# Larger batches in an attention and Fourier kernel: five and six steps, one of them held back through SBUF

## The chip, the cores and the metric

One core of a Trainium2 chip. The metric is the device time of one launch in microseconds (us), the median of three runs. Engines as the profile names them: PE is TensorE's matmul (PEld its weight load), DVE VectorE, ACT ScalarE, POOL GpSimd, SP SyncE.

## The reference

Two independent parts, joined on the last axis. A is attention with 16 query heads of 28 and a single key and value head; B is a Fourier filter over both axes of a 2048 x 448 array.

```python
q = (x @ wq).reshape(B, S, H, Dh).transpose(0, 2, 1, 3)     # S 2048, D 448, H 16, Dh 28
k, v = x @ wk, x @ wv
p = softmax(einsum("bhqd,bkd->bhqk", q, k) * Dh ** -0.5)
a = einsum("bhqk,bkd->bhqd", p, v).transpose(0, 2, 1, 3).reshape(B, S, H * Dh) @ wo
y = irfft2(rfft2(x2) * (w_r + 1j * w_i))
return concatenate([a, y], axis=-1)
```

## The kernel before

The first 70 us project queries, keys and values and do the first Fourier stage; the change does not touch them. Then comes the loop. Queries are cut into four column blocks `c` of 512 and the heads into four groups `g` of four, keys into 16 blocks `kc` of 128. A **step** is one (c, g, kc): 256 in all. It has four **scores** (L780), one 128x512 matmul into a PSUM bank for each head of the group, four exps on ScalarE (L781) from the bank into a buffer `p` in SBUF, and the **value products** in `flush` (L756), four matmuls of 32 columns of `vs` that lie side by side in TensorE's array, accumulated over the 16 steps of a group in one bank `po`. In the trace a value product has two records, so eight a step. The sums of the exps come along as row 28 of each head's 32 rows.

The steps come in **batches** (`PLAN`): the scores of all steps of a batch, then the value products of the steps that are old enough. `KEEP = 2` says that two steps stay pending. Pieces of other work, **units**, are written into the score part: A and B (`fft2_a`, `fft2_b`, three matmuls L519 to L521 each: second Fourier stage), Z (`fft3_a`, `fft3_b`: third stage), W (`wo_unit`, L677: output projection), F (the end of the first stage). The batch lists are A, B, BACK (three steps and a unit), CHUNK (four steps and four W), PAIR and ONE.

Eight PSUM banks serve scores, units and `po`. TensorE's and VectorE's orders are the order of the program text (`manual_schedule`), ScalarE's is left to the scheduler. `take` hands out the oldest free bank, and a score must wait until its bank's last exp or copy is through.

VectorE copies the units' results out of PSUM, makes the products with the filter in `fft2_a` (L565 to L568) and splits them into a high and a low part (`ph`, `pl`), builds the next query block (`build_q`), splits the output weights (`wo_split`) and divides by the softmax sums (`norm`): a copy of `po`, then four times a shuffle that spreads row 28 over the 32 rows, a reciprocal over 128 columns, a product and a high and low part.

Of the kernel before, what the change touches and what calls it, by code (L numbers as in the profile page):

```python
# [21 lines left out]
DH = D // H  # L22
# [10 lines left out]
P_BUFS = 12  # L33
# [4 lines left out]
def batch(*units):  # L38

    return [("----" + u) if i else ("---" + u + "-") for i, u in enumerate(units)]  # L40
# [8 lines left out]
ROOM = {"A": 0, "B": 2, "W": 2, "Z": 2, "": 1, "F": 0}  # L49

KEEP = 2
# [4 lines left out]
def kernel(ctx: ExitStack, tc: tile.TileContext, t: dict):  # L56
# [139 lines left out]
    def build_q(c, g, first=False):  # L196
        cs = slice(c * CW, (c + 1) * CW)
        qh = qp.tile([128, CW], F32R, name="qh", bufs=1)
        ql = qp.tile([128, CW], F32R, name="ql", bufs=1)
        qt = ql.bitcast(F32)  # L200
        nc.vector.tensor_scalar(qt, qraw[:, g, cs], mask, cvec[:, g, c:c + 1], op0=ALU.mult, op1=ALU.add)
        nc.vector.tensor_copy(qh, qt)
        nc.vector.tensor_tensor(ql, qt, qh.bitcast(F32), op=ALU.subtract)
        if (c, g) not in qa:
            qa[c, g] = qp.tile([128, 4, CW], F32R, name="qa")
        q = qa[c, g]
        if first:
            return q, qh, ql
        for i in range(4):
            for p, src in enumerate((qh, ql)):  # L210
                mv = nc.sync.dma_start(q[32 * p:32 * p + 32, i].bitcast(F32), src[32 * i:32 * i + 32].bitcast(F32))
                behind(mv, stored[-1])
        nc.sync.dma_start(q[64:128].bitcast(F32), q[0:64].bitcast(F32))
# [263 lines left out]
    ctx.enter_context(tc.manual_schedule(engines={mybir.EngineType.DVE}))  # L477
# [5 lines left out]
    take, late = free.popleft, []  # L483

    def give(bank, scores=1):

        late.append([scores, bank])

    def scored(bank):
        free.append(bank)  # L490
        for x in late:
            x[0] -= 1
        free.extend(bank for n, bank in late if n == 0)
        late[:] = [x for x in late if x[0]]
    ap = pools.enter_context(tc.tile_pool(name="ap", bufs=2))
    pp = pools.enter_context(tc.tile_pool(name="pp", bufs=P_BUFS))

# [12 lines left out]
    def wo_split(g):  # L510
        if g >= NG:
            nc.vector.tensor_copy(wox[:, g - NG], wo[g])
            return
        nc.vector.tensor_copy(woh[:, g], wo[g])
        nc.vector.tensor_tensor(wol[:, g], wo[g], woh[:, g].bitcast(F32), op=ALU.subtract)

# [28 lines left out]
    def fft2_split(u):  # L545
        q, v = divmod(u, 2)
        b = b2["b", q][:, 2 * v:2 * v + 2]
        bh = b2["h", u] = fp.tile([128, 2, DF], F32R, name="bh", bufs=1)
        nc.vector.tensor_copy(bh, b.bitcast(F32))
        nc.vector.tensor_tensor(b, b.bitcast(F32), bh.bitcast(F32), op=ALU.subtract)  # L550

    def fft2_a(u):
        q, v = divmod(u, 2)
        s = slice(2 * v, 2 * v + 2)
        b, wr, wi = (b2[n, q][:, s] for n in ("b", "wr", "wi"))
        bank = take()
        pu = halves2(bank)
        mm3(pu, "g1", b2["h", u], b)
        us = fp.tile([128, 2, DF], F32, name="us", tag="us", bufs=1)
        nc.vector.tensor_copy(us, pu)  # L560
        give(bank)
        if u < 15:
            fft2_split(u + 1)
        pf, p2 = fp.tile([128, 2, DF], F32, name="pwr"), fp.tile([128, 2, DF], F32, name="pwi")
        nc.vector.tensor_tensor(pf, us, wr, op=ALU.mult)  # L565
        nc.vector.tensor_tensor(p2[0:64], us[64:128], wi[64:128], op=ALU.mult)
        nc.vector.tensor_tensor(p2[64:128], us[0:64], wi[0:64], op=ALU.mult)
        nc.vector.scalar_tensor_tensor(pf, p2, sgn, pf, op0=ALU.mult, op1=ALU.add)  # L568
        h = fp.tile([128, 2, DF], F32R, name="ph")
        nc.vector.tensor_copy(h, pf)  # L570
        p = fp.tile([128, 2, DF], F32R, name="pl")
        nc.vector.tensor_tensor(p, pf, h.bitcast(F32), op=ALU.subtract)
        pr[u] = h, p

    def fft2_b(u):
        v = u % 2
        bank = take()
        pc = halves2(bank)
        mm3(pc, "g2", *pr.pop(u))
        if v == 0:  # L580
            cst[0] = fp.tile([128, 4, DF], F32, name="cst")
        nc.vector.tensor_copy(cst[0][:, 2 * v:2 * v + 2], pc)
        give(bank)
# [22 lines left out]
    def fft3_a(q, e):  # L606
# [3 lines left out]
        for j in range(4):  # L610
            mm(pz[:w, j], c2["c", q][:, j, o0:o0 + w], c2["F", q][:, j], start=True, stop=True)  # L611
        z = c2["z", q, e] = fp.tile([113, 2, 4, 64], F32, name=f"z{e}", tag=("wi", "cst")[e])
        nc.vector.tensor_copy(z[:w], pz[:w].rearrange("p j (r n) -> p r j n", r=2))
        give(bank)

    def fft3_b(q, v):
# [5 lines left out]
        for k, (z, w, r) in enumerate(((ze, 113, 0), (zo, 112, 0), (zo, 112, 1), (ze, 113, 1))):  # L622
            mm(py[:, k], z[:w, r, js], cs3[:w, k], start=True, stop=True)  # L623
        m = fp.tile([128, 4, 113], F32, name="m", tag="us", bufs=1)
        nc.vector.tensor_copy(m, py)  # L625
        give(bank)
        y1 = fp.tile([128, 2, 2, 113], F32, name="y1", tag="pwr")
        nc.vector.tensor_tensor(y1[:, :, 0], m[:, 0:2], m[:, 2:4], op=ALU.add)
        nc.vector.tensor_tensor(y1[:, :, 1], m[:, 0:2], m[:, 2:4], op=ALU.subtract)
        yo = fp.tile([128, 4, 113], F32, name="yo", tag="pwi")  # L630
        nc.gpsimd.tensor_tensor(yo[:, 0:2], y1[:, 0], y1[:, 1], op=ALU.add)  # L631
        nc.gpsimd.tensor_tensor(yo[:, 2:4], y1[:, 0], y1[:, 1], op=ALU.subtract)
        r0 = (2 * q + v) * 128
        nc.sync.dma_start(t["ob"][r0:r0 + 128], yo)
# [14 lines left out]
    def norm(c, g, k):  # L649

        if k == 0 and g == 0:
            oh[c] = pp.tile([128, NG, CW], F32R, name="oh", bufs=1)
            ol[c] = pp.tile([128, NG, CW], F32R, name="ol", bufs=1)
        s = slice(128 * k, 128 * k + 128)
        o = osb[c, g][:, s]
        r = ap.tile([128, 128], F32, name="r", bufs=1)
        nc.vector.stream_shuffle(r, o, [DH] * 32)
        nc.vector.reciprocal(r, r)  # L658
        if c < NC - 1:
            nc.vector.tensor_tensor(o, o, r, op=ALU.mult)  # L660
        else:
            nc.vector.scalar_tensor_tensor(o, o, mask, r, op0=ALU.mult, op1=ALU.mult)
        if (c, g) == (NC - 1, NG - 1):
            return
        h = oh[c][:, g, s]
        nc.vector.tensor_copy(h, o)
        nc.vector.tensor_tensor(ol[c][:, g, s], o, h.bitcast(F32), op=ALU.subtract)
        if k == 3 and c < NC - 1:
            spares(c, g)
# [9 lines left out]
    def wo_out(p, c, k, on_act=False):  # L679
# [3 lines left out]
        else:  # L683
            nc.vector.tensor_copy(y, p)  # L684
        r0 = c * CW + k * 128
# [4 lines left out]
    def wo_unit(c, k, g):  # L690
        if g == 0:
            wps[c, k] = take()
        p = wps[c, k][:, :D]
        wo_mm(p, c, k, (g,))
        if g == NG - 1:
# [17 lines left out]
    place, where, room = [], {}, []  # L713
    for b, steps in enumerate(PLAN):
        for i, s in enumerate(steps):
            for k in s.replace("-", ""):
                where.setdefault(k, []).append(len(place))
            place.append((b, i))
        units = "".join(steps).replace("-", "")
        room.append(ROOM[units[:1]])  # L720
# [14 lines left out]
    builds = set()  # L735
    for g in range(NC * NG - 1):
        n = next(n for n in range(16 * g + 3, 16 * g + 13) if place[n][1] < 2 and room[place[n][0]])
        builds.add(n)
        room[place[n][0]] -= 1

# [6 lines left out]
    pend, po = [], {}  # L747
    step = 0

    def flush(keep, last=False):  # L750
        while len(pend) > keep:
            c, g, kc, ps = pend.pop(0)
            if kc == 0:
                po[c, g] = take()
            for i in range(4):
                mm(po[c, g][32 * i:32 * i + 32], vs[:, kc], ps[i // 2][:, i % 2], start=(kc == 0), stop=(kc == 15))  # L756
            if kc == 15:
                o = osb[c, g] = ap.tile([128, CW], F32, name="osb")
                if last:
                    for k in range(4):  # L760
                        s = slice(128 * k, 128 * k + 128)
                        nc.scalar.activation(o[:, s], po[c, g][:, s], AF.Copy)
                else:
                    nc.vector.tensor_copy(o, po[c, g])
                    give(po[c, g])
                    norms.extend((c, g, k) for k in range(4))

    for c, g in order:
        for kc in range(16):
            ps, n = [], 0  # L770
            b, i = place[step]
            for k in PLAN[b][i]:
                if k != "-":
                    f, *a = todo[k].popleft()
                    f(*a)
                    continue
                if n % 2 == 0:
                    ps.append(pp.tile([128, 2, CW], F32, name="p"))
                sc = take()
# [238 lines left out]
```

## Time and profile before

| | |
|---|---|
| median of 3 runs | 651.04 us (650.68 to 651.18) |
| profiled execution: span | 649.8 us |
| TensorE, matmul busy | 642.6 us |
| ScalarE busy | 555.9 us |
| VectorE busy | 360.5 us |
| GpSimd busy | 79.6 us |
| granted TensorE clock | full in every slice |

Busy times are unions of overlapping records; matmuls are pipelined, so the time from one start to the next is what an instruction costs, not its own length. In the chain of work that ended last, a row gives start, length, engine, tile, line and count. In a timeline row the bracket at the end gives the idle time before and what ended it. A row of a group gives busy time and the mean of one in ns, then idle time before it and who ended that.

### The profile page before, as it was taken

How to read it: one execution, taken by the hardware profiler on the slowest of the kernel's cores; microseconds unless marked ns; L12 is line 12 of the kernel's file. 1: busy time of each engine (PE TensorE's matmuls, PEld its weight loads, DVE VectorE, ACT ScalarE, POOL GpSimd, SP SyncE). 2: the span in 40 equal slices, each digit the busy share in tenths (PEclk: the TensorE clock that was granted, in tenths of full speed). 3: DMA queues.
4: the chain of work that ended last, by engine and by line, in shares of the span. 5: the costliest groups of instructions: out<-in, count | busy, mean ns of one | idle time of the engine just before them, and what ended most of it. 6: DMA issues, size and time to landing. Idle time of an engine off the chain costs nothing.

```text
span 649.8 us, 12076 instructions
## 1 busy us (share of the span) xinstructions
PE 642.6 (99%) x4470; PEld 375.8 (58%) x4470; DVE 360.5 (55%) x810; ACT 555.9 (86%) x1103; POOL 79.6 (12%) x150
## 2 busy tenths in 40 slices
PE   8999999999999999999999999999999999999996
PEld 6877554555555456554546556565656565555555
DVE  5999646778877771047765620175443510383523
ACT  5654999999999998789989988799999987899981
POOL 3022401101112100000012200011120200010010
PEclk9999999999999999999999999999999999999999
DMA  8756954534552443022062323032232313140001
GB/s 268 265 172 165 259 159 106 137 100 121 138 139 76 109 95 84 29 75 49 32 155 50 98 60 89 20 88 73 63 94 61 101 39 84 43 110 16 15 31 60
DMA packets 36114, 63.83 MB, mean 98 GB/s; under 512 B 7905, under 2 KB 23922, under 8 KB 35084
## 3 DMA queue, kind: packets, MB, share of 16 engines
q1 hardware_dynamic: 30832, 49.60, 27.6%
q0 software_dynamic: 4640, 12.48, 7.4%
q8 instruction: 36, 0.59, 0.4%
q10 hardware_dynamic: 576, 0.92, 0.4%
q14 instruction: 30, 0.25, 0.1%
HBM read 30.04 MB, written 14.75 MB: 69 GB/s over the span
## 4 chain that ended last, share of the span: by engine, by line
PE 98%; DMA 1%; ACT 0%; SPq 0%; ACTq 0%; issue 0%
PE s L780 30%; PE s L756 24%; PE po L756 7%; PE s L331 6%; PE sx L780 5%; PE po L780 4%; PE sx L756 4%; PE s L677 4%; PE s L138 2%; PE s L623 2%; PE s L611 1%; PE pbb L157 1%; DMA raw<-wq 1%; PE s L521 1%; PE s L519 1%; PE s L520 1%
## 5 line engine op out<-in xcount | busy, mean ns | idle before, releaser
L781 ACT ACTIVATE p<-s 128x512 f32<-128x512 f32 x776 | 421.9, 652 | 38.8 <-PE s L780 38.5
L780 PE MATMUL s<-qa,ka 128*128 128x512 f32 x776 | 243.8, 408 | 0.0
L780 PEld LDWEIGHTS s<-qa,ka 128*128 128x128 f32 x776 | 140.3, 188 | 80.5 <-ACT p L781 43.6
L756 PE MATMUL s<-p,vs 128*32 128x512 f32 x1408 | 163.8, 596 | 0.0
L756 PEld LDWEIGHTS s<-p,vs 128*32 128x32 f32 x1408 | 39.7, 109 | 89.5 <-issue 86.6
L781 ACT ACTIVATE p<-sx 128x512 f32<-128x512 f32 x132 | 86.1, 652 | 3.4 <-PE sx L780 3.4
L781 ACT ACTIVATE p<-po 128x512 f32<-128x512 f32 x116 | 74.9, 646 | 7.2 <-PE po L780 7.1
L658 DVE RECIPROCAL r<-r 128x128 f32<-128x128 f32 x64 | 61.0, 953 | 2.2
L684 DVE COPY ya<-s 128x448 f32<-128x448 f32 x11 | 6.9, 625 | 88.1 <-PE s L677 88.1
L780 PE MATMUL sx<-qa,ka 128*128 128x512 f32 x132 | 53.4, 405 | 0.0
L780 PE MATMUL po<-qa,ka 128*128 128x512 f32 x116 | 47.4, 408 | 0.0
L756 PE MATMUL po<-p,vs 128*32 128x512 f32 x384 | 44.9, 597 | 0.0
L631 POOL TENSOR_TENSOR yo<-y 128x226 f32<-128x226 f32 x16 | 9.6, 597 | 225.9 <-issue 214.8
L780 PEld LDWEIGHTS sx<-qa,ka 128*128 128x128 f32 x132 | 24.8, 188 | 14.0 <-ACT p L781 9.2
L647 POOL DMA_DIRECT2D ol<-ol x36 | 18.1, 508 | 105.4 <-PE s L780 55.9
L756 PE MATMUL sx<-p,vs 128*32 128x512 f32 x256 | 29.7, 596 | 0.0
L780 PEld LDWEIGHTS po<-qa,ka 128*128 128x128 f32 x116 | 21.8, 188 | 12.4 <-ACT p L781 7.0
L625 DVE COPY m<-s 128x452 f32<-128x452 f32 x15 | 9.4, 629 | 34.5 <-PE s L623 34.5
L756 PEld LDWEIGHTS po<-p,vs 128*32 128x32 f32 x384 | 10.7, 109 | 24.1 <-issue 23.4
L331 PE MATMUL s<-xh,wqh 128*128 128x512 f32 x56 | 22.7, 405 | 0.9 <-ACT wqh L311 0.9
L335 ACT ACTIVATE qraw<-s 128x512 f32<-128x512 f32 x14 | 8.1, 600 | 17.4 <-PE s L331 17.4
L331 PE MATMUL s<-xh,wql 128*128 128x512 f32 x56 | 21.6, 391 | 0.0
(211 smaller groups left out, 735.3 us busy)
## 6 DMA issues: line engine op xcount, KB each, us to landing
qa<-qa SPq DMA_DIRECT2D x15, 512.0 KB
raw<-xa SPq DMA_DIRECT2D x16, 256.0 KB
xb<-xb SPq DMA_DIRECT2D x8, 512.0 KB
qa<-qh SPq DMA_DIRECT2D x64, 64.0 KB
qa<-ql SPq DMA_DIRECT2D x60, 64.0 KB
ob<-yo SPq DMA_DIRECT2D x16, 226.0 KB
t<-bs SPq DMA_DIRECT2D x16, 225.0 KB
wr<-wr POOLq DMA_DIRECT2D x16, 225.0 KB, 4.4
```

The lines of the kernel that those rows point to most:

```text
L138: mm(pa[r0:r0 + 32, e, o0:o0 + n], f[:, 2 * r + k, 2 * p + e, h], cs1[:, 2 * r + k, :n], start=True, stop=True)
L331: mm(pq, w[:, j, gs], x[:, j], start=(j == 0 and n == 0), stop=(j == 3 and n == 1))
L335: out = nc.scalar.activation(qraw[:, g, cs], pq, AF.Copy)
L623: mm(py[:, k], z[:w, r, js], cs3[:w, k], start=True, stop=True)
L625: nc.vector.tensor_copy(m, py)
L631: nc.gpsimd.tensor_tensor(yo[:, 0:2], y1[:, 0], y1[:, 1], op=ALU.add)
L647: nc.gpsimd.dma_start(ol[c][o, g].bitcast(F32), ol[c][r, 0].bitcast(F32))
L658: nc.vector.reciprocal(r, r)
L677: mm(p, x[c][:, g, s], w, start=(g == 0 and n == 0), stop=(g == NG - 1 and n == 2))
L756: mm(po[c, g][32 * i:32 * i + 32], vs[:, kc], ps[i // 2][:, i % 2], start=(kc == 0), stop=(kc == 15))
L780: begun.append(mm(sc, ka[:, kc * 128:(kc + 1) * 128], qa[c, g][:, n], start=True, stop=True))
L781: nc.scalar.activation(ps[-1][:, n % 2], sc, AF.Exp, scale=SCALE)
```

## The change

- `PLAN`: 86 batches become 49. After two batches of one step and four of two, eleven have five steps, 31 have six, and the last has five. A token `-` is a score as before, `k` or `e` one of the last step's four scores, letters are units (`X` is four W, `Y` two Z).
- The last step of a batch of five or six (`k`): VectorE copies the score bank to SBUF (`keep`), and ScalarE does the exps there later, two instructions of 128x1024, behind the exps of the batch. In the batches of one and two steps (`e`) ScalarE takes them from PSUM.
- `flush` comes once a batch: the first step, the step kept from the batch before, then the others. The batch's last step is kept. `P_BUFS` goes from 12 to 8, beside four buffers `k`.
- ScalarE's order is now the program's too. Banks are handed out by clocks that the program keeps for three engines (`clock`, `passed`, `at_once`).
- VectorE's work that nobody waits for at once goes through two queues (`put`, `pop`, `need`) and is issued when VectorE's kept clock is not ahead of TensorE's.
- In `fft2_a` the two half-height products go to GpSimd.
- The division: `po` is transposed in 32x32 blocks on the way out of PSUM, so that a query's sum lies beside its 28 values; one reciprocal over 16 columns, one product, and a transpose back.

```diff
-A, B, BACK = [batch(u, "", "") for u in "ABZ"]
-CHUNK = 4 * [4 * ["--W--"]]
-ONE, PAIR = batch(""), batch("", "")
-PLAN = ([["----F"], ONE] + 4 * [PAIR] + [batch("A", ""), A] + 11 * [B, A] + [PAIR] + CHUNK
-        + 3 * [B, A] + [B, B, PAIR, ONE] + 6 * [BACK] + CHUNK + [PAIR] + 15 * [BACK] + CHUNK + 11 * [BACK])
+PLAN = ["eeeeF", "eeee"] + 4 * [spread(2, "", 0)]
+PLAN += ["-k-k-k-k----------A--"] + [spread(5, u) for u in ["A"] + 9 * ["BA"]]
+PLAN += [spread(6, u) for u in ["BA"] + 4 * ["WBWA"] + 2 * ["WBW"] + ["X"]]
+PLAN += [spread(6, u) for u in 5 * ["Y"] + 4 * ["X"] + 6 * ["Y"] + 4 * ["X"]]
...
+    def passed(work):
+        clock["pe"] += work
+        while any(queue) and clock["dve"] <= clock["pe"]:
+            pop()
+        clock["dve"] = max(clock["dve"], clock["pe"] - 512)
...
         us = fp.tile([128, 2, DF], F32, name="us", tag="us", bufs=1)
         nc.vector.tensor_copy(us, pu)
...
-        nc.vector.tensor_tensor(p2[0:64], us[64:128], wi[64:128], op=ALU.mult)
-        nc.vector.tensor_tensor(p2[64:128], us[0:64], wi[0:64], op=ALU.mult)
+        nc.gpsimd.tensor_tensor(p2[0:64], us[64:128], wi[64:128], op=ALU.mult)
+        nc.gpsimd.tensor_tensor(p2[64:128], us[0:64], wi[0:64], op=ALU.mult)
...
+    def divide(c, g, k=None):
...
+            r = osb["r"] = ap.tile([128, 16], F32, name="r", bufs=1)
+            nc.vector.reciprocal(r, sums[:, :, DH])
...
+        put(("o", c, g), [lambda: divide(c, g), lambda: nc.vector.transpose(o, o),
+                          lambda: nc.vector.tensor_copy(h, o), rest], 640)
...
+            c, g, kc = steps[i if kind == "-" else n - 1]
+            sc = take()
+            begun.append(mm(sc, ka[:, kc * 128:(kc + 1) * 128], qa[c, g][:, h], start=True, stop=True))
+            passed(232)
+            if kind == "-":
+                waiting.append((sc, new[i], h))
+                exps()
+            elif k == "k":
+                nc.vector.tensor_copy(keep[h // 2][:, h % 2], sc)
+                at_once()
+                give(sc)
+                lazy.append(h)
...
+        flush(steps[:1] + kept if n > 4 else kept + steps[:-1], steps[1:-1] if n > 4 else [])
+        kept = steps[-1:]
...
+            for p in keep:
+                nc.scalar.activation(p, p, AF.Exp, scale=SCALE)
```

How the orders move. TensorE, in the A and B batches, before: scores (`s`, `sx`, `po` are banks), a B unit (L519 to L521) and the value products (L756) of three steps.

```order
L520 MATMUL po<-ph,g2l 128x450
L521 MATMUL po<-pl,g2h 128x450
L780 MATMUL s_88<-qa,ka 128x512
L780 MATMUL s_85<-qa,ka 128x512
L780 MATMUL s_89<-qa,ka 128x512
L780 MATMUL sx<-qa,ka 128x512
L780 MATMUL s_86<-qa,ka 128x512
L780 MATMUL s_87<-qa,ka 128x512
L780 MATMUL s_88<-qa,ka 128x512
L780 MATMUL po<-qa,ka 128x512
L780 MATMUL s_85<-qa,ka 128x512
L756 MATMUL s_84<-p,vs 32x512 x12
```

Twelve scores and one unit lie between two runs of value products. The same place in the new order, the end of a batch of five (scores are L875, value products L830, an A unit L557 to L559):

```order
L557 MATMUL sx<-bh,g1h 128x450
L558 MATMUL sx<-bh,g1l 128x450
L559 MATMUL sx<-b_1709,g1h 128x450
L875 MATMUL s_85<-qa,ka 128x512
L875 MATMUL s_87<-qa,ka 128x512
L875 MATMUL s_88<-qa,ka 128x512
L875 MATMUL s_86<-qa,ka 128x512
L875 MATMUL sx<-qa,ka 128x512
L830 MATMUL s_84<-p,vs 32x512 x4
L830 MATMUL s_84<-k,vs 32x512 x4
L830 MATMUL s_84<-p,vs 32x512 x12
```

Twenty scores, a B and an A unit lie between two runs, and a run takes the first step, the kept one (`k`) and three more. The same batch earlier, from its eighth score (the fourth `k`, in bank `po`):

```order
L875 MATMUL po<-qa,ka 128x512
L875 MATMUL s_89<-qa,ka 128x512
L557 MATMUL s_85<-ph,g2h 128x450
L558 MATMUL s_85<-ph,g2l 128x450
L559 MATMUL s_85<-pl,g2h 128x450
L875 MATMUL sx<-qa,ka 128x512
L875 MATMUL s_87<-qa,ka 128x512
L875 MATMUL s_88<-qa,ka 128x512
L875 MATMUL s_86<-qa,ka 128x512
L875 MATMUL s_89<-qa,ka 128x512
L875 MATMUL po<-qa,ka 128x512
```

The bank that VectorE copies last is asked for again by the fifteenth score. VectorE in another batch of five, behind its four score copies (L881), the B unit's copy (`cst`) and the first half of a weight split:

```order
L554 TENSOR_TENSOR wol<-wo,woh 128x448
L602 COPY us<-s_86 128x450
L610 TENSOR_TENSOR pwr<-us,wr 128x450
L588 CAST bh<-b_1484 128x450
L589 TENSOR_TENSOR b_1484<-b_1484,bh 128x450
L614 SCALAR_TENSOR_TENSOR pwr<-pwi,sgn,pwr 128x450
L615 CAST ph<-pwr 128x450
L616 TENSOR_TENSOR pl<-pwr,ph 128x450
L834 STREAM_TRANSPOSE osb<-sx 128x512
L711 RECIPROCAL r<-osb 128x16
L716 TENSOR_TENSOR osb<-osb,r 128x512
L730 STREAM_TRANSPOSE osb<-osb 128x512
```

The two products that stood between L610 and L614 are gone to GpSimd (`pwi`), a division stands behind the unit's chain, and the next batch's copies follow it.

More of the change, by code (lines that the diff above doesn't have):

```diff
@@ L576, in fft2_b @@
         v = u % 2
+        need(("pr", u))
         bank = take()
@@ L732 @@
         at(max(where["Z"][4 * q] - 8, where["B"][-1] + 1), fft3_load, q)
[L735 to L739, printed above, removed]
     norms = deque()
@@ L798 @@
     while norms:
         norm(*norms.popleft())
+    while any(queue):
+        pop()
     c = NC - 1
```

302 lines of the change are left out of this document (186 added, 116 removed).

## Prediction

> **What bounds the kernel now.** I read the page's busy shares first, then the chain of work that ended last.
>
> ```profile
> span 649.8 us, 12076 instructions
> PE 642.6 (99%) x4470; PEld 375.8 (58%) x4470; DVE 360.5 (55%) x810; ACT 555.9 (86%) x1103; POOL 79.6 (12%) x150
> PE 98%; DMA 1%; ACT 0%; SPq 0%; ACTq 0%; issue 0%
> ```
>
> The third row is the chain: TensorE is on it for 98% of the span, so a change pays only if TensorE has less to do or waits less. Busy time does not say whether it runs at its rate, so the next view is the timeline of its matmuls.
>
> ```profile
> 321.42 0.37 PE L519 MATMUL s<-ph,g2h 128*128 128x450 f32 x1
> ...
> 322.03 0.40 PE L780 MATMUL sx<-qa,ka 128*128 128x512 f32 x1
> 322.26 1.33 PE L780 MATMUL s<-qa,ka 128*128 128x512 f32 x5
> 323.43 0.40 PE L780 MATMUL sx<-qa,ka 128*128 128x512 f32 x1
> ```
>
> Five scores take 323.43 - 322.26 = 1.17 us, so 0.234 each; three 450-column matmuls take 322.03 - 321.42 = 0.61. Now the chain in order of time, which shows the value products (L756, eight records a step):
>
> ```profile
> 92.39 1.85 PE s L756 x16
> 97.91 2.71 PE s L756 x24
> 100.62 0.43 PE s L780
> ...
> 249.88 3.57 PE s L756 x32
> 259.63 3.57 PE s L756 x32
> ...
> 317.98 2.71 PE po L756 x24
> 324.30 2.71 PE po L756 x24
> ...
> 620.06 0.88 PE s L623 x8
> ...
> 629.67 4.43 PE s L756 x40
> ```
>
> Two, three, four and five steps cost 1.85, 2.71, 3.57 and 4.43 us: 0.86 a step and a constant of 0.13. The first score behind them takes 0.43 in place of 0.234, another 0.20. A Z unit (L623) takes 0.88. So each run of value products costs **0.33 us** that does no work. The periods agree: a batch of three with one A or B unit is 12 x 0.234 + 0.61 + 3 x 0.86 = 6.00, and the period is 324.30 - 317.98 = 6.32; a batch of four with its eleven output matmuls (L677, taken at the same 0.203) is 3.74 + 2.23 + 3.44 = 9.41, and the period is 9.75. What is left over is 0.32 and 0.34. TensorE waits for nobody in these batches; its only waste is the toll.
>
> **The change part by part.** *Fewer runs.* The old plan has 86 batches and leaves up to two steps pending; its first batch has nothing old enough, so there are 85 runs of L756. The new plan has 49 batches and holds back one step; its first flush is empty and the last follows a run directly, so 48 runs. Scores, units and value products stay in number: 1024 scores, 256 steps, 16 A, 16 B, 48 W, 32 Z. Gain: 37 x 0.33 = **12.2 us**.
>
> *ScalarE.* It must keep up with fewer gaps. A row of exps, and its only instruction of 1024 columns:
>
> ```profile
> 258.23 1.18 ACT L781 ACTIVATE p<-s 128x512 f32<-128x512 f32 x2
> 259.18 0.72 ACT L781 ACTIVATE p<-sx 128x512 f32<-128x512 f32 x1
> 259.66 1.22 ACT L781 ACTIVATE p<-s 128x512 f32<-128x512 f32 x2
> ```
>
> ```profile
> L250 ACT ACTIVATE ka<-kf x1: 1046/1046/1046, 42.4 to 42.4; 32x1024 fp32r<-32x1024 f32 x1
> ```
>
> Three exps start in 259.66 - 258.23 = 1.43 us, 0.477 each. An exp over 1024 columns from SBUF has no row; it lies between two exps back to back, 0.954, and the 1024-column copy with nothing overlapped, 1.046. A new batch of five needs 16 x 0.477 + 2 x 1.046 = 9.7 us at most, against TensorE's 20 x 0.234 + 5 x 0.86 + 2 x 0.61 + 0.33 = 10.5; of six with two Z units 11.6 against 5.6 + 5.2 + 1.8 + 0.3 = 12.9. The deferred exps lie under the value products: in a five-step batch these last 4.4 us, and two of 1.046 follow some four leftover exps (1.9), 4.0 in all. If that cover were gone, the excess of each batch would be paid. I take nothing. The eight score buffers `p` (twelve before) hold four steps; in a six-step batch the fifth step's exps wait for the first step's value product, which is why that one goes first, 3.4 us ahead of the fifth's own. Nothing either.
>
> *VectorE, the term against.* It gains four copies of 128x512 out of PSUM in 43 batches, loses two of its three products per A unit to GpSimd, and its softmax division shrinks.
>
> ```profile
> L658 DVE RECIPROCAL r<-r 128x128 f32<-128x128 f32 x64 | 61.0, 953 | 2.2
> L657 DVE STREAM_SHUFFLE r<-osb 128x128 f32<-128x128 f32 x64 | 19.1, 298 | 0.0
> L764 DVE COPY osb<-s 128x512 f32<-128x512 f32 x10 | 6.9, 690 | 14.7 <-PE s L756 14.7
> L203 DVE TENSOR_TENSOR ql<-ql,qh 128x512 fp32r<-128x512 f32 x16 | 11.3, 709 | 0.5
> ```
>
> The reciprocal over 128 columns four times a group becomes one over 16 columns, about 16/128 x 0.95 = 0.12. The two 32x32 transposes of 128x512 have no row. Below stands the copy at 0.69, above the reciprocal's rate, 4 x 0.95 = 3.8; nearest is the shuffle, which also moves data between partitions and takes 0.298 for 128 columns, the time of a plain elementwise operation of that size. I take 0.65. The freed time lies off the chain and buys nothing by itself. What counts is where VectorE must answer: TensorE wants the copied banks back. The chain of an A unit before:
>
> ```profile
> 108.56 0.63 DVE L560 COPY us<-s 128x450 f32<-128x450 f32 x1 [0.80 <-ACT p L781]
> 109.10 0.39 DVE L549 CAST bh<-b 128x450 fp32r<-128x450 f32 x1
> 109.52 0.63 DVE L550 TENSOR_TENSOR b<-b,bh 128x450 fp32r<-128x450 f32 x1
> 110.07 0.62 DVE L565 TENSOR_TENSOR pwr<-us,wr 128x450 f32<-128x450 f32 x1
> 110.72 0.62 DVE L566 TENSOR_TENSOR pwi<-us,wi 64x450 f32<-64x450 f32 x1
> 111.37 0.62 DVE L567 TENSOR_TENSOR pwi<-us,wi 64x450 f32<-64x450 f32 x1
> 112.03 0.69 DVE L568 SCALAR_TENSOR_TENSOR pwr<-pwi,sgn,pwr 128x450 f32<-128x450 f32 x1
> 112.75 0.40 DVE L570 CAST ph<-pwr 128x450 fp32r<-128x450 f32 x1
> 113.18 0.63 DVE L572 TENSOR_TENSOR pl<-pwr,ph 128x450 fp32r<-128x450 f32 x1
> ```
>
> By starts: the PSUM copy costs 0.54 (its tail overlaps; a 512-column one 0.60), the three operations before the two moved products 0.42 + 0.55 + 0.65 = 1.62, the three behind them 0.72 + 0.43 + 0.63 = 1.78. In the new order L614 stands behind the first three and waits for GpSimd. GpSimd's price:
>
> ```profile
> L631 POOL TENSOR_TENSOR yo<-y x16: 577/584/813, 355.9 to 629.2; 128x226 f32<-128x226 f32 x16
> ```
>
> ```profile
> 355.88 0.81 POOL L631 TENSOR_TENSOR yo<-y 128x226 f32<-128x226 f32 x1 [6.03 <-DVE y L629]
> 356.29 0.69 DVE L202 CAST qh<-ql 128x512 fp32r<-128x512 f32 x1
> 356.66 0.76 POOL L632 TENSOR_TENSOR yo<-y 128x226 f32<-128x226 f32 x1
> 357.01 0.96 DVE L203 TENSOR_TENSOR ql<-ql,qh 128x512 fp32r<-128x512 f32 x1
> ```
>
> At 0.584 for 226 columns, 450 take about 1.1, two 2.2: if nothing interferes, L614 starts 2.3 us after `us` and the chain behind `us` is 2.3 + 1.8 = 4.1 us, against 4.7 before. But the last four rows show the two engines stretching each other: L203 took 0.96 where its mean is 0.71, GpSimd 0.81 and 0.76 where alone it takes 0.58. Run strictly in turn (product 0.65, GpSimd 1.1, cast 0.40, GpSimd 1.1, difference 0.55) the chain is 3.8 + 1.8 = 5.6.
>
> Now the slack. From a batch's first score: the second score's result is there at 0.43 + 0.40 = 0.83, four copies at 0.60 end at 3.2. The fourth copied bank is asked for again behind fourteen scores and B: 0.43 + 13 x 0.234 + 0.61 = 4.1 (`po` in the new TensorE order shown with the change). So a lag up to 0.8 us is free. The batch whose VectorE order is shown with the change: copies to 3.2, `cst` 3.8, a weight split 0.42 + 0.57 to 4.8; `us` waits for A until 5.1 and ends at 5.6; the chain to 9.7 or 11.2; transpose 0.65, reciprocal 0.12, product 0.70, transpose 0.65 to 11.8 or 13.3. The next copies are due at 10.5 + 0.8 = 11.3, so the lag is 0.5 or 2.0 and TensorE stands 0 or 1.2 us. Six of the eleven five-step batches carry such an extra load (a division, a query build or a weight split); counted likewise with full turns they cost 0.3 to 1.4 each, 5.7 together, and 0 with none. Six-step batches add 1.8 us of TensorE time each and absorb it. The rows show stretching, but over pieces only, so I take the middle: **+3 us**, bounds 0 and 5.7.
>
> A rule of the Trainium skill speaks against the move to GpSimd: the page "SBUF — State Buffer", section "Who interferes with whom", says that a VectorE instruction with two SBUF inputs and a GpSimd instruction that reads SBUF exclude each other for the whole instruction. By that rule the cost is the 5.7 end, not 3; the four rows above agree in kind, and only one such meeting is in this trace.
>
> *Start and tail.* The eight-score batches at the start keep their size, and the tail from 629.67 + 4.43 = 634.1 runs the same output matmuls; the last division is ready under the partial sums. Nothing.
>
> Sum: 649.8 - 12.2 + 3.0 = 640.6 us of span. The runs' median is 1.2 above the profiled span (651.04 against 649.8), so **641.8 us**.
>
> **The rivals.** *No stall*: GpSimd's products hide, 649.8 - 12.2 + 1.2 = 638.8. For it: VectorE was busy only 55% of the span. Against: the stretched rows.
>
> *VectorE and GpSimd take turns*: 638.8 + 5.7 = 644.5, up to 647 if the six-step A batches lag by the same half microsecond. The rule quoted above would give this. For it: L203 at 0.96. Against: the overlap there is one meeting.
>
> *The toll is no toll but ScalarE's late release, which grows with the batch.* The page puts the idle weight loads of the scores down to ScalarE:
>
> ```profile
> L780 PEld LDWEIGHTS s<-qa,ka 128*128 128x128 f32 x776 | 140.3, 188 | 80.5 <-ACT p L781 43.6
> ```
>
> If that were the cause, the loss would go with the exps, 85 x 0.33 = 28 us over 256 steps, and longer batches would save none of it: 651.0 + 3 = 654, slower. It decides as soon as the toll of a six-step batch exceeds (28 - 3) / 48 = 0.52 us. Against: runs of two to five steps all show 0.13 + 0.20, and while weight loads stand idle the array is still streaming.
>
> *Slow transposes.* At 3.8 us instead of 0.65, the seven transposes in the five-step batches add 22 us that VectorE, full there, can't hide: 641.8 + 22 = 664. It decides (no gain left) from 0.65 + 9.2 / 7 = 2.0 us each. Against: the shuffle's 0.298.
>
> **How the numbers follow.** Forecast, 640 to 643.5: 0.48. No stall, 638 to 640: 0.20. Turns, 643.5 to 648: 0.20. Toll that grows 0.05, slow transposes 0.04, something within 0.2% of before 0.03. About 0.2% is what a measurement of this kernel can tell from no change. Faster 0.88, same 0.03, slower 0.09. The range 638 to 647 leaves out the slower cases and the end of the turns.
>
> **What would show it.** The chain of waits should list about 48 runs of value products, periods of 10.5 us (A and B), 12.9 (Z) and the same 0.33 left over. The exp over 1024 columns should be near 0.95 and end before the next batch. The transposes near 0.65. A score waiting for VectorE in the batches between 95 and 210 us, of 0.5 to 1.4 us, confirms the term of 3; none there confirms the first rival. Waits for ScalarE in the Z batches, or a first score behind a run that takes much more than 0.43, would make the prediction wrong.

## The result, and the profile after

| | median of its runs | range | runs |
|---|---|---|---|
| before | 651.09 us | 650.58 to 651.58 | 12 |
| changed | 650.75 us | 649.82 to 651.92 | 12 |

The ratio is 0.9994, 95% interval 0.9986 to 1.0002: no change that can be measured. The prediction was 641.8 us with a range of 638 to 647, so it was wrong. Its gain of some 12 us did come, and nearly all of it went out again in three places.

From the page of the changed kernel: span, busy times, the chain that ended last, and three groups (line, engine, operation, shapes, count, then busy time and mean of one in ns, then the idle time before them).

```profile
span 649.4 us, 12044 instructions
PE 639.5 (98%) x4470; PEld 381.7 (59%) x4470; DVE 386.4 (59%) x663; ACT 552.6 (85%) x1013; POOL 121.1 (19%) x182
PE 90%; DVE 7%; DMA 1%; ACT 1%; issue 1%; SPq 0%; ACTq 0%; DVEq 0%
L898 ACT ACTIVATE k<-k 128x1024 f32<-128x1024 f32 x86 | 88.1, 1103 | 0.0
L606 POOL TENSOR_TENSOR pwi<-us,wi 64x450 f32<-64x450 f32 x16 | 23.2, 1448 | 113.3 <-DVE us L602 76.3
L834 DVE STREAM_TRANSPOSE osb<-s 128x512 f32<-128x512 f32 x11 | 7.9, 715 | 38.8 <-PE s L830 38.8
```

TensorE's busy time fell by 3.1 us, the span by 0.4. VectorE, which was not in the chain, now holds 7% of it. The two new operations have the size that was assumed: the transpose 0.715 us (0.65 assumed), and of two 1024-column exps in a row the second starts 0.95 us behind the first (0.95 to 1.05 assumed). GpSimd's products took 1.45 us each (L606), not the 1.1 assumed, and the reciprocal over 16 columns 0.25 (L711, below), not 0.12.

The groups of VectorE, by line:

```profile
L589 DVE TENSOR_TENSOR b<-b,bh 128x450 fp32r<-128x450 f32 x16 | 18.3, 1146 | 0.6
L588 DVE CAST bh<-b 128x450 fp32r<-128x450 f32 x16 | 17.8, 1111 | 0.0
```

These two stand beside the products that moved to GpSimd. Before, the same cast took 0.39 us and the same difference 0.63 in the unit that the prediction showed. What this does to TensorE, from the timelines of TensorE and of VectorE around two of the five-step batches:

```profile
122.98 0.63 PE L875 MATMUL s<-qa,ka 128*128 128x512 f32 x2
124.16 0.50 PE L875 MATMUL s<-qa,ka 128*128 128x512 f32 x1 [0.55 <-DVE k L881]
```

```profile
138.03 0.63 DVE L602 COPY us<-s 128x450 f32<-128x450 f32 x1 [0.35 <-PE s L559]
...
139.24 1.35 DVE L588 CAST bh<-b 128x450 fp32r<-128x450 f32 x1
140.63 1.46 DVE L589 TENSOR_TENSOR b<-b,bh 128x450 fp32r<-128x450 f32 x1
...
143.70 0.71 DVE L834 STREAM_TRANSPOSE osb<-sx 128x512 f32<-128x512 f32 x1
144.44 0.25 DVE L711 RECIPROCAL r<-osb 128x16 f32<-128x16 f32 x1
...
146.09 2.45 DVE L881 COPY k<-s 128x512 f32<-128x512 f32 x4
```

The first fence has a score that starts 1.18 us behind a pair that should take 0.47: it waits for the first of its own batch's four copies to free a bank (that copy ends at 124.11). The second, two batches later, shows how such copies come late: the cast and the difference last 2.8 us together, the division follows, and the four copies of a batch whose first score starts at 143.58 begin at 146.09.

For the whole loop I took, from the matmul starts, each period between two runs of value products and subtracted its work at the prediction's prices (0.234 a score, 0.203 a unit's matmul, 0.88 a Z unit, 0.86 a step, 0.33 toll). What is left, in us, with four of the experiments below beside it (rounding of the prices moves a whole column by up to half a microsecond; differences between columns hold to about 0.2):

| batches | before | changed | e1 | e2 | e6 | e12 |
|---|---|---|---|---|---|---|
| 11 of five steps, A and B | | 6.4 | 2.3 | 6.4 | 1.9 | 0.8 |
| 6 of six steps, A or B and W | | 2.5 | 2.5 | 2.5 | 2.5 | 0.9 |
| 9 of six steps, W | | 0.9 | 0.8 | 0.9 | 0.8 | -0.2 |
| 16 with Z | | 2.5 | 2.6 | 1.1 | 1.1 | -0.2 |
| whole loop | 1.0 | 12.4 | 8.3 | 11.0 | 6.4 | 1.3 |

The loop has 48 runs of value products as predicted, and 37 fewer are worth 37 x 0.33 = 12.2. But waits rose from 1.0 to 12.4 us, 11.4 more. The experiments say what each part of these 11.4 is.

### The profile page after: what moved, and what is told of

Same layout as the page of the kernel before. It is cut to its first block, busy times and chain, and to the rows that moved or that the text cites. A ratio compares the mean times of both kernels' runs of the same rounds, so it can differ in the third digit from the quotient of the medians.

```text
span 649.4 us, 12044 instructions
## 1 busy us (share of the span) xinstructions
PE 639.5 (98%) x4470; PEld 381.7 (59%) x4470; DVE 386.4 (59%) x663; ACT 552.6 (85%) x1013; POOL 121.1 (19%) x182
## 4 chain that ended last, share of the span: by engine, by line
PE 90%; DVE 7%; DMA 1%; ACT 1%; issue 1%; SPq 0%; ACTq 0%; DVEq 0%
PE s L875 28%; PE s L830 22%; PE po L830 6%; PE s L343 6%; PE sx L875 4%; PE po L875 4%; PE s L739 3%; PE sx L830 3%; PE s L141 2%; PE s L672 2%; PE s L658 1%; PE sx L739 1%; PE po L739 1%; DVE bh L588 1%; PE pbb L160 1%; DVE k L881 1%
## 5 line engine op out<-in xcount | busy, mean ns | idle before, releaser
L819 ACT ACTIVATE p<-s 128x512 f32<-128x512 f32 x645 | 344.6, 631 | 40.4 <-PE s L875 33.4
L875 PE MATMUL s<-qa,ka 128*128 128x512 f32 x786 | 238.3, 408 | 2.1 <-DVE k L881 2.1
L875 PEld LDWEIGHTS s<-qa,ka 128*128 128x128 f32 x786 | 144.4, 188 | 76.3 <-issue 30.5
L830 PE MATMUL s<-p,vs 128*32 128x512 f32 x1136 | 134.1, 595 | 0.0
L881 DVE COPY k<-s 128x512 f32<-128x512 f32 x122 | 78.1, 680 | 75.9 <-PE s L875 75.7
L898 ACT ACTIVATE k<-k 128x1024 f32<-128x1024 f32 x86 | 88.1, 1103 | 0.0
L830 PEld LDWEIGHTS s<-p,vs 128*32 128x32 f32 x1136 | 34.4, 109 | 75.1 <-issue 72.2
L819 ACT ACTIVATE p<-sx 128x512 f32<-128x512 f32 x95 | 59.9, 630 | 4.1 <-PE sx L875 3.1
L819 ACT ACTIVATE p<-po 128x512 f32<-128x512 f32 x88 | 55.8, 634 | 6.4 <-PE po L875 4.7
L875 PE MATMUL sx<-qa,ka 128*128 128x512 f32 x121 | 48.8, 403 | 0.0
L875 PE MATMUL po<-qa,ka 128*128 128x512 f32 x117 | 47.4, 405 | 0.0
L606 POOL TENSOR_TENSOR pwi<-us,wi 64x450 f32<-64x450 f32 x16 | 23.2, 1448 | 113.3 <-DVE us L602 76.3
L881 DVE COPY k<-po 128x512 f32<-128x512 f32 x27 | 18.4, 681 | 41.2 <-PE po L875 41.2
L830 PE MATMUL po<-p,vs 128*32 128x512 f32 x312 | 37.2, 595 | 0.0
L830 PE MATMUL s<-k,vs 128*32 128x512 f32 x272 | 35.6, 594 | 0.0
L875 PEld LDWEIGHTS po<-qa,ka 128*128 128x128 f32 x117 | 22.0, 188 | 10.2 <-issue 3.4
L875 PEld LDWEIGHTS sx<-qa,ka 128*128 128x128 f32 x121 | 22.7, 188 | 8.3 <-issue 3.4
L830 PE MATMUL sx<-p,vs 128*32 128x512 f32 x208 | 24.8, 595 | 0.0
L881 DVE COPY k<-sx 128x512 f32<-128x512 f32 x23 | 15.6, 680 | 14.1 <-PE sx L875 14.0
```

The source lines that it names most:

```text
L606: nc.gpsimd.tensor_tensor(p2[0:64], us[64:128], wi[64:128], op=ALU.mult)
L819: nc.scalar.activation(tiles[-1][:, h % 2], sc, AF.Exp, scale=SCALE)
L875: begun.append(mm(sc, ka[:, kc * 128:(kc + 1) * 128], qa[c, g][:, h], start=True, stop=True))
L881: nc.vector.tensor_copy(keep[h // 2][:, h % 2], sc)
L898: nc.scalar.activation(p, p, AF.Exp, scale=SCALE)
```

## The experiments

Theory at the outset: VectorE and GpSimd take turns (A and B batches), a bank is held too long in the Z batches, and the last scores of a batch run short of banks. The main rival was that fewer runs of value products save little. Every ratio is to the kernel before on the same chip.

**e1: the half-height products back on VectorE.**

```diff
-        nc.gpsimd.tensor_tensor(p2[0:64], us[64:128], wi[64:128], op=ALU.mult)
-        nc.gpsimd.tensor_tensor(p2[64:128], us[0:64], wi[0:64], op=ALU.mult)
...
+            lambda: nc.vector.tensor_tensor(p2[0:64], us[64:128], wi[64:128], op=ALU.mult),
+            lambda: nc.vector.tensor_tensor(p2[64:128], us[0:64], wi[0:64], op=ALU.mult)], first=True)
```

> The changed kernel with one thing undone: the two half-height filter products of an A unit go back from GpSimd to VectorE (into the same queue as the third product). Theory 'turns': the 8.9 us that the A and B batches lose (11 five-step batches 0.58 us each above their work, six with W 0.41) come from VectorE and GpSimd excluding each other, L588 and L589 taking 1.3 us in place of 0.4 and 0.6. Then the chain behind us shrinks from about 5.6 to 4.7 us although VectorE does 1.3 us more, the five-step batches go to 10.6 us on average, and the time falls by 5 to 8 us, to 643 to 646. Rival 'load': VectorE is simply full there and the exclusion is hidden; then 1.3 us more per A unit costs 10 us or more, time 660 and up.

Measured: 646.45 us, ratio 0.993 (0.9914 to 0.9947). VectorE does two products more for each A unit, and the kernel is 4.3 us faster. The same stretch of its timeline:

```profile
136.22 0.63 DVE L602 COPY us<-s 128x450 f32<-128x450 f32 x1 [0.35 <-PE s L559]
...
138.79 0.40 DVE L588 CAST bh<-b 128x450 fp32r<-128x450 f32 x1
139.23 0.63 DVE L589 TENSOR_TENSOR b<-b,bh 128x450 fp32r<-128x450 f32 x1
...
142.82 2.48 DVE L882 COPY k<-s 128x512 f32<-128x512 f32 x4
```

The copies start 6.6 us after `us`; in the changed kernel it is 146.09 - 138.03 = 8.1. In the table only the row of the five-step batches falls, by 4.1. VectorE has more work and TensorE waits less, so the turns are shown and the rival 'load' is out; the gain is a little under the 5 to 8 us that were expected.

**e2: `m`, the copy of a Z unit's bank, in two buffers.** A Z unit's copy then need not wait for the additions (`y`) of the unit before it.

```diff
-        need(("y", 2 * q + v - 1))
-        m = fp.tile([128, 4, 113], F32, name="m", tag="us", bufs=1)
+        need(("y", 2 * q + v - 2))
+        m = fp.tile([128, 4, 113], F32, name="m", tag="ph")
```

> The changed kernel, with two buffers in place of one for the tile m into which the fft3_b units are copied, so that the second Z unit's copy need not wait for the queue to be worked off to the first one's sums. Theory 'held bank': the 2.5 us that the 15 six-step Z batches lose come from those with fft3_b units, where the second unit's bank was copied 2.4 us late and the last scores ran at the pace of ScalarE's releases (0.49 us each); the time falls by about 2.5 us. Rival 'ScalarE's pace': eight banks less po are too few for six steps whatever VectorE does; the last scores of the Z batches still stand at 0.49 and the time stays within 0.7 us.

Measured: 649.36 us, ratio 0.9972 (0.9962 to 0.9982), 1.4 less than the change. VectorE behind the two Z units of one batch, in the changed kernel and then in e2:

```profile
467.78 0.63 DVE L676 COPY m<-s 128x452 f32<-128x452 f32 x1 [0.32 <-PE s L672]
468.32 0.68 DVE L209 TENSOR_TENSOR ql<-ql,qh 128x512 fp32r<-128x512 f32 x1
...
470.81 0.63 DVE L676 COPY m<-sx 128x452 f32<-128x452 f32 x1
```

```profile
466.89 0.63 DVE L676 COPY m<-s 128x452 f32<-128x452 f32 x1 [0.32 <-PE s L672]
...
468.03 0.62 DVE L676 COPY m<-sx 128x452 f32<-128x452 f32 x1
```

The second unit's bank comes back 1.1 us after the first's and not 3.0: with one buffer, `need` issued everything that was queued ahead of the additions. The Z row of the table falls from 2.5 to 1.1, where the expectation had all of it go. The rest has another cause.

**e3: the products on GpSimd in the kernel before, nothing else.**

```diff
-        nc.vector.tensor_tensor(p2[0:64], us[64:128], wi[64:128], op=ALU.mult)
-        nc.vector.tensor_tensor(p2[64:128], us[0:64], wi[0:64], op=ALU.mult)
+        nc.gpsimd.tensor_tensor(p2[0:64], us[64:128], wi[64:128], op=ALU.mult)
+        nc.gpsimd.tensor_tensor(p2[64:128], us[0:64], wi[0:64], op=ALU.mult)
```

> The kernel before with one part of the change alone: the two half-height products on GpSimd. Measures the price of the exclusion where TensorE's plan has no score copies. Both theories: L549, L550 or L565 beside a product take 1.2 to 1.5 us in place of 0.4 to 0.6 and GpSimd's product 1.2 to 1.6. Theory 'turns': VectorE's chain per A unit grows by 0.5 to 1 us, and since nothing in that plan asks VectorE for score banks, the time stays within 1.5 us of before. Rival 'load': VectorE is relieved by 1.3 us an A unit and its chain is shorter; time also same. The chain's length tells them apart: above or below 4.7 us from the end of us to the end of pl.

Measured: 652.14 us, ratio 1.0014 (1.0004 to 1.0023). The timeline of both engines:

```profile
110.10 1.24 POOL L566 TENSOR_TENSOR pwi<-us,wi 64x450 f32<-64x450 f32 x1 [6.82 <-DVE us L560]
...
110.35 1.47 DVE L550 TENSOR_TENSOR b<-b,bh 128x450 fp32r<-128x450 f32 x1
...
111.42 1.42 POOL L567 TENSOR_TENSOR pwi<-us,wi 64x450 f32<-64x450 f32 x1
111.75 1.57 DVE L565 TENSOR_TENSOR pwr<-us,wr 128x450 f32<-128x450 f32 x1
```

GpSimd's first product ends at 111.34, and L550, in its place since 110.35, ends 0.48 later, less than the 0.63 that it takes alone. L567 then runs to 112.84, and L565 ends 0.48 after that again. The chain from the end of `us` (110.02) to the end of `pl` (115.21) takes 5.2 us, against 4.6 in the prediction's rows of the kernel before. The turns belong to the move and not to the new plan. In the old plan, with three steps and one unit a batch, they cost about 1 us (0.3 to 1.5 by the interval); with five steps and two units 4.3.

**e4: no copies, every score's exp out of PSUM.**

```diff
-def spread(n, units, lazy=4, start=0.9, rest=0.85):
+def spread(n, units, lazy=0, start=0.9, rest=0.85):
...
-PLAN += ["-k-k-k-k----------A--"] + [spread(5, u) for u in ["A"] + 9 * ["BA"]]
+PLAN += [spread(5, "A")] + [spread(5, u) for u in ["A"] + 9 * ["BA"]]
```

> The changed kernel without the held step's copies: the last step's four scores are exponentiated from PSUM as the others, in the same batches of five and six. Theory: the copies are what lets batches grow, since seven banks hold seven scores while value products run; without them a six-step batch needs 17 exps before its last score, 17 x 0.477 + 0.5 = 8.6 us against 7.3 of score part, and ScalarE idles about 2 us under the value products; 1.2 us per six-step batch and 0.6 per five-step, some 44 us, less the VectorE lag of 9 that goes with the copies: 680 to 690. Rival: VectorE's copies cost more than they give, ScalarE keeps up by itself; time under 650.

With `lazy=0` the last step's four scores also move from between the first ones to the end of the batch. Measured: 710.75 us, ratio 1.0913 (1.0894 to 1.0931), a loss of 60 us, where 680 to 690 us had been expected. The end of a Z batch's scores on TensorE:

```profile
527.32 0.50 PE L875 MATMUL sx<-qa,ka 128*128 128x512 f32 x1
527.80 0.50 PE L875 MATMUL s<-qa,ka 128*128 128x512 f32 x1
528.24 1.07 PE L830 MATMUL s<-p,vs 128*32 128x512 f32 x8
```

The last scores start 0.48 apart, ScalarE's pace for one exp and twice TensorE's own 0.234. So the copies carry long batches: without them the same plan loses 60 us.

**e5: e1 and e2 together.**

> The two edits that helped, together: the products on VectorE, and two buffers for m. If they are separate losses the gains add: 4.3 and 1.4 us below the changed kernel's 650.75, 645.0. If both only uncover the same shortage of banks, the second adds less than 0.5 us to the first: 646.0 to 646.4.

Measured: 644.6 us, ratio 0.9902 (0.9886 to 0.9919). Changed minus 4.3 minus 1.4 is 645.0, so the two causes are separate.

**e6: e5 with the units of the ten five-step batches earlier.**

```diff
-PLAN += ["-k-k-k-k----------A--"] + [spread(5, u) for u in ["A"] + 9 * ["BA"]]
+PLAN += ["-k-k-k-k----------A--"] + [spread(5, u, 4, 0.5) for u in ["A"] + 9 * ["BA"]]
```

> As the one before, and in nine five-step batches the B and A units stand two scores earlier. Theory 'shortage': each run of value products now costs 0.43 us in place of 0.33 because the batch's last score takes the bank that the A unit used, which VectorE frees 0.24 us after its weights could have been loaded; with A 0.5 us earlier that wait goes, 0.1 us in nine batches, and the interval from the last score to the value products falls from 0.43 to 0.33; time 1 us lower than the one before. Rival 'length': the larger toll belongs to longer batches or to value products that read two kinds of buffers; the intervals stay at 0.43 and the time within 0.4 us.

Measured: 643.74 us, ratio 0.9886 (0.987 to 0.9903), 0.9 us less than e5. The end of the same batch's scores on TensorE, in e5 (with the weight load of the last score) and then in e6:

```profile
136.64 0.19 PEld L876 LDWEIGHTS s<-qa,ka 128*128 128x128 f32 x1 [0.23 <-DVE us L602]
136.64 0.50 PE L876 MATMUL s<-qa,ka 128*128 128x512 f32 x1
137.07 1.07 PE L831 MATMUL sx<-p,vs 128*32 128x512 f32 x8
```

```profile
136.99 1.32 PE L876 MATMUL s<-qa,ka 128*128 128x512 f32 x5
138.25 1.07 PE L831 MATMUL s<-p,vs 128*32 128x512 f32 x8
```

In e5 the first value product starts 0.43 after the last score; in e6 it is 138.25 - 136.99 - 4 x 0.234 = 0.32, as before the change. The wait is that of a last score for its bank, which the copy `us` of the A unit frees (0.23 in the weight load's row), and it shows up as a late value product. That the time agrees with the expected 1 us is in part luck: from the first to the last run of value products e6 takes 548.7 us and e5 549.0. The nine batches with B and A together lose 0.9 us less, as expected, but the first of the ten, which holds an A unit alone, loses 0.5 more; the other 0.5 us lies before the loop and behind the last matmul, which the edit does not touch.

**e7: the changed kernel with its Z batches in threes, one Z unit each.** This asks whether fewer runs of value products save what was counted.

```diff
-PLAN += [spread(6, u) for u in 5 * ["Y"] + 4 * ["X"] + 6 * ["Y"] + 4 * ["X"]]
+PLAN += [spread(6, u) for u in []]
+PLAN += 10 * [spread(3, "Z")] + 4 * [spread(6, "X")] + 12 * [spread(3, "Z")] + 4 * [spread(6, "X")]
...
-PLAN += [spread(6, "Y")] * (left // 6) + [spread(left % 6, "Y")] * (left % 6 > 0)
+PLAN += 8 * [spread(3, "Z")] + [spread(left - 24, "Y")]
```

> The changed kernel with its fifteen six-step Z batches cut into thirty of three steps (one Z unit each, the last step's scores still copied). Theory 'toll': fifteen more runs of value products at 0.33 us cost 5.0, and the 2.5 us that the long Z batches lose to waits come back; time 2.5 us above the changed kernel, 653, each batch of three 6.6 us long. Rival 'no toll' (the loss goes with exps, not with runs): the time falls by the waits alone, 648.

Measured: 652.9 us, ratio 1.0029 (1.0016 to 1.0042). Fifteen more runs cost 15 x 0.33 = 5.0, the Z batches' waits of 2.5 vanish (under 0.1 left), and 2.2 slower was measured. The toll is what it was taken for.

**e8: the new division in the kernel before, nothing else.**

```diff
-        nc.vector.stream_shuffle(r, o, [DH] * 32)
-        nc.vector.reciprocal(r, r)
...
+            nc.vector.reciprocal(r, sums[:, :, DH])
...
+        nc.vector.transpose(o, o)
...
-                    nc.vector.tensor_copy(o, po[c, g])
+                    nc.vector.transpose(o, po[c, g])
```

> The kernel before with the new division alone (po transposed on its way out, one reciprocal over 16 columns, product, transpose back in four pieces; the last group as before). Theory: VectorE's time there is off the chain; its busy time falls by some 60 us and the time stays within 0.7 us of 651.0. Rival: VectorE's release of banks was holding TensorE somewhere in the old plan, time 1 us or more lower.

Measured: 650.74 us, ratio 0.9995 (0.9986 to 1.0005). From its page:

```profile
PE 642.8 (99%) x4470; PEld 375.8 (58%) x4470; DVE 304.6 (47%) x663; ACT 555.9 (86%) x1103; POOL 79.5 (12%) x150
```

VectorE lost 360.5 - 304.6 = 55.9 us of work and the time stayed: nobody waited for it.

**e9 and e10: e6 with the units of the six mixed batches earlier, and with A and B ahead of W.**

```diff
-PLAN += [spread(6, u) for u in ["BA"] + 4 * ["WBWA"] + 2 * ["WBW"] + ["X"]]
+PLAN += [spread(6, "BA")] + [spread(6, u, 4, 0.5) for u in 4 * ["WBWA"] + 2 * ["WBW"]] + [spread(6, "X")]
```

In e10 the lists read `BAWW` and `BWW`.

> The version of e6 with the units of the six six-step batches that hold A or B work started earlier as well (the spacing table alone is changed; work is the same). Bank shortage at the batch's end: these six batches now lose 0.41 us each, 2.5 in all, in scores that wait for a bank behind the last unit and in value products whose weights come late; with the last unit further from the end the loss falls to 0.1 to 0.2 each, 641.9 to 642.6 us against e6's 643.74. Rival, VectorE or ScalarE is simply full there: the loss stays in another place, 643.4 to 644.1, and the interval from the last score to the first value product may fall while scores in mid-batch wait instead.

> As e9, but in these six batches A and B come ahead of the two W units. Bank shortage: a W unit gives its bank back after one addition on VectorE, without GpSimd or a chain behind it, so A and B first is at least as good, 641.7 to 642.6 us. Full engine: 643.4 to 644.1, as in e9. If the B unit comes too early behind its A unit's chain, B waits for VectorE by 0.5 to 1 us in each of four batches, 644 to 646.

Measured: 643.59 us, ratio 0.9883 (0.9866 to 0.9899), and 644.33 us, ratio 0.9894 (0.9878 to 0.9911). The rival holds: the waits of these batches stay (2.4 and 3.5 us) and only change their place. e10 lies in the range named for a B unit that waits for VectorE, but TensorE's list of waits has no such wait. Its premise did not hold either: a W unit gives no bank back at once. The first of four W units takes the bank and the fourth gives it back (`wo_unit`), so with two W in a batch it stays out from one batch into the next. In the changed kernel the three batches that end with it out lose 0.5 to 0.6 us each, the three that give it back 0.2 to 0.35; this fits a shortage of banks, but no run tests it. TensorE and ScalarE at the end of one of the six in e9:

```profile
281.03 0.50 PE L876 MATMUL sx<-qa,ka 128*128 128x512 f32 x1
281.52 0.50 PE L876 MATMUL s<-qa,ka 128*128 128x512 f32 x1
```

```profile
276.46 4.02 ACT L820 ACTIVATE p<-s 128x512 f32<-128x512 f32 x8
280.27 0.70 ACT L820 ACTIVATE p<-sx 128x512 f32<-128x512 f32 x1
280.75 1.69 ACT L820 ACTIVATE p<-s 128x512 f32<-128x512 f32 x3
283.11 1.08 ACT L820 ACTIVATE p<-s 128x512 f32<-128x512 f32 x2 [0.67 <-PE po L831]
...
285.03 2.02 ACT L899 ACTIVATE k<-k 128x1024 f32<-128x1024 f32 x2
```

ScalarE is without a gap to the end of the scores, and the last ones start 0.49 apart, at its pace. Its 0.67 of idleness comes only behind them (the eight buffers `p` are full) and costs nothing, as its work ends at 287.1, with the value products.

**e11 and e12: is it ScalarE's pace?** Both are e6 with the eight buffers `p` taken once and used in turn, filled with ones by GpSimd before the loop; in e12 the exps cover 384 of 512 columns (the other 128 columns of `p` keep their ones, so e12 leaves out a quarter of these exps).

```diff
+    ring = deque(pp.tile([128, 2, CW], F32, name=f"p{i}", bufs=1) for i in range(P_BUFS))
+    for p in ring:
+        nc.gpsimd.memset(p, 1.0)
...
-                tiles.append(pp.tile([128, 2, CW], F32, name="p"))
+                tiles.append(ring[0])
+                ring.rotate(-1)
...
-            nc.scalar.activation(tiles[-1][:, h % 2], sc, AF.Exp, scale=SCALE)
+            nc.scalar.activation(tiles[-1][:, h % 2, :384], sc[:, :384], AF.Exp, scale=SCALE)
```

> The version of e6 with the eight buffers p taken once and used in turn, each filled with ones by GpSimd before the loop; nothing else. Control for the next run. Expected 643.7 us as e6, plus up to 1 if GpSimd's fills come in the way at the start of the loop.

> The control with the exps out of PSUM over 384 of the 512 columns (the computation of the other 128 columns of each such score is left out; their place in p holds ones; scores, value products and copies keep their size). ScalarE's pace is what still costs time: the trace of e6 has 6.4 us of waits in the loop, and with exps a fifth shorter the banks come back sooner and the waits fall under 2 us: 638.5 to 640.5. Rival, VectorE's answers or TensorE's own order cost it: the waits stay, within 0.7 us of the control.

Measured: 651.8 us, ratio 1.0008 (0.9998 to 1.0017), and 646.37 us, ratio 0.9931 (0.9914 to 0.9948). The control is 8.1 slower than e6, far more than expected, before the loop and not in it (the last section says why); its loop has e6's 6.4 us of waits. Beside it, e12 is 5.4 us faster (not at the expected 638.5 to 640.5, since the control is slower too), and its waits are 1.3, near the 1.0 of the kernel before. One group of e12's ScalarE:

```profile
L821 ACT ACTIVATE p<-s 128x384 f32<-128x384 f32 x608 | 269.0, 509 | 86.7 <-PE s L880 66.4 <-PE s L832 12.9 <-ACT p L821 3.6
```

The end of the scores of one mixed batch, first in e11 (the weight loads of the last two scores and the first value product), then in e12 (the last two scores and the first value product):

```profile
289.31 0.19 PEld L880 LDWEIGHTS sx<-qa,ka 128*128 128x128 f32 x1 [0.30 <-ACT p L821]
289.80 0.19 PEld L880 LDWEIGHTS s<-qa,ka 128*128 128x128 f32 x1 [0.30 <-ACT p L821]
290.23 1.06 PE L832 MATMUL s<-p,vs 128*32 128x512 f32 x8
```

```profile
287.12 0.39 PE L880 MATMUL sx<-qa,ka 128*128 128x512 f32 x1
287.36 0.40 PE L880 MATMUL s<-qa,ka 128*128 128x512 f32 x1
287.68 1.06 PE L832 MATMUL s<-p,vs 128*32 128x512 f32 x8
```

In e11 the last two scores wait for ScalarE's exps and stand 0.49 apart; in e12 they stand 0.24 apart and the value product follows at 0.32. VectorE's work, the units and TensorE's order are the same in both. With faster exps the waits fall in all four rows of the table, so ScalarE's pace inside the scores is what they hung on.

## Why the prediction was wrong, step by step

- **The gain of 12.2 us from 37 runs fewer: right.** 48 runs, the same 0.33 each (e7).
- **VectorE's +3 (0 to 5.7): right in mechanism, undersized.** e1 shows 4.3. As argued, the loss falls in some of the five-step batches (five of them lose 0.3 to 1.2 us of it), and the cause is the turns, not VectorE's load. The Trainium skill's page "SBUF — State Buffer", section "Who interferes with whom", says that a VectorE instruction with two SBUF inputs and a GpSimd instruction that reads SBUF exclude each other; e3's rows agree (0.63 us alone, 1.47 and 1.57 beside a product). The rival that took this rule at its word had 5.7, the forecast 3; the measured 4.3 lies between. That six-step batches absorb it held: e1 left their row at 2.5.
- **"Six-step batches add 1.8 us of TensorE time each and absorb it": wrong for the Z batches.** The step looked at VectorE's total and not at what one `need` issues ahead of a copy; a bank held for it cost 1.4 (e2).
- **"ScalarE ... I take nothing": this is the step that failed most.** It compared ScalarE's work and TensorE's time over a whole batch (9.7 against 10.5). But banks fill and empty within the scores. A six-step Z batch has 24 x 0.234 + 1.8 = 7.4 us of scores and units; ScalarE starts some 0.8 late and can begin (7.4 - 0.8) / 0.477 = 14 exps in them. Of its 20, six are left in banks and one or two run, out of seven banks beside `po`. That is just at the limit, so the last scores begin to wait for ScalarE. The term that was put at nothing measured 5.1 us (e6 to e12: 6.4 to 1.3). Without it the changed kernel would have taken an estimated 650.75 - 5.1 = 645.6 us; the 5.1 was measured on e6's version, not on the changed kernel itself. It is 0.1 us a batch on average but uneven: 1.6 us in the six mixed batches, 1.1 in the five-step ones (nearly all in the first two), 1.0 in the nine with W, 1.3 in the sixteen with Z. The count above is of a Z batch and is worked out, not measured; what the mixed batches add to it was not counted.
- **The new operations, the division, the eight buffers: right but for the reciprocal (0.25 us, not 0.12).** e8 shows that the division buys nothing by itself, and in e9 the full buffers stop ScalarE only where nobody waits.
- **What would have shown it wrong was named, but not where it lay.** Waits for ScalarE do not stand under that name in TensorE's list of matmul waits. They stand in the rows of its weight loads, but so do 43.6 us in the kernel before that cost nothing (the row that the prediction shows). What tells them apart is a value product that starts 0.43 after the last score, not 0.33, and last scores 0.49 apart.

The account from the span before: 649.8 - 12.2 + 4.1 (turns) + 1.4 (Z's bank) + 0.5 (units too near the end of a batch: 12.4 - 4.1 - 1.4 = 6.9 against e6's 6.4) + 5.1 (ScalarE's pace) = 648.7, against 649.4. Of the 0.7 that is left, 0.3 are waits of the loop that no experiment took away; 0.4 stays open.

The best version found is e9 with 643.59 us, or e6 with 643.74, which this measurement cannot tell apart: the change without its move to GpSimd, with the second buffer for `m` and the units earlier, 1.2% faster than before.

## What to carry to other kernels

Longer batches save a fixed toll for each switch, but whether the engines keep up must be asked where banks are scarce, at the end of the scores, and not over a whole batch. Moving elementwise work to GpSimd to relieve VectorE lost 4.3 us here with VectorE busy 59% and GpSimd 19% of the span, because VectorE's next instructions read SBUF too. A new limit of about 0.1 us a batch appears in no list of matmul waits; it shows when the interval between two starts is compared with the same interval before.

## What was not expected of the hardware

GpSimd's eight fills held up one VectorE cast for their whole length. VectorE's and then GpSimd's row of e11 before the loop:

```profile
66.86 8.09 DVE L196 CAST qa<-qh 32x512 fp32r<-32x512 f32 x2
```

```profile
67.01 7.22 POOL L858 MEMSET p<- 128x1024 f32 x8
```

The same two casts in e6, and then the chain of work of e11 in order of time, which tells the two apart:

```profile
66.65 0.83 DVE L196 CAST qa<-qh 32x512 fp32r<-32x512 f32 x2
```

```profile
66.94 7.57 DVE qa L196
...
74.52 0.42 DVE qa L196
```

The first cast waits; the second, when the fills are over, takes 0.42 us, as in e6. The two end 0.7 us after the last of the eight fills, which only write SBUF. The Trainium skill's page "SBUF — State Buffer", section "Who interferes with whom", says that a VectorE cast in a mode with two ports and GpSimd block each other for a whole instruction. The first row agrees, though no row says in which mode the cast ran, and shows more: the cast got no turn between eight fills either. The wait is in the chain with 7.57 us, some 7.2 more than the cast takes otherwise, and e11's loop starts 8.1 us later than e6's (first value product at 81.42 and 73.30). From 66 to 80 us TensorE's granted clock was 0.80 in e11 and 1.00 in e6, which may hold the rest; no run separates the two. In the changed kernel the cast L588, with one SBUF input, was likewise stretched to 1.35 us.
